# RWKV attention and a maxout layer on one core: the weights' upper halves cast by GpSimd into dense words, the first keys placed by VectorE, the squares of the first chunks taken at the end

## The chip, the cores and the metric

The kernel runs on one core of one Trainium2 chip. The metric is the device time of one execution in microseconds; lower is better.

## The reference

A linear attention with decay (batch 4, 8 heads, 768 tokens, 48 features a head) feeds a feed-forward layer that takes the maximum of three products:

```python
for t in range(S):
    kt, vt, rt = (k[:, :, t], v[:, :, t], r[:, :, t])
    cur = np.einsum('bhd,bhe->bhde', u[None] * kt, vt)
    y[:, :, t] = np.einsum('bhd,bhde->bhe', rt, state + cur)
    state = w[None, :, :, None] * state + np.einsum('bhd,bhe->bhde', kt, vt)
...
x = np.ascontiguousarray(attn_out.transpose(0, 2, 1, 3)).reshape(B * S, H * D)
h = np.maximum(np.maximum(x @ w1, x @ w2), x @ w3)
return (h @ w_out).astype(np.float32)
```

x is 3072 x 384, w1 to w3 are 384 x 768 and w_out is 768 x 384, all four in 64-bit floats; r, k and v are 32-bit.

## The kernel before, in words

**Staging.** The tokens go in 12 chunks of 64 (for all 4 batches, so 256 columns a chunk). A chunk's attention goes in two halves q of 4 heads. For each half SyncE loads `feat` (keys and receptances with the features on partitions) and `tok` (k, r, v with the tokens on partitions). The decay is folded in by scaling `feat`. TensorE makes `scores` (keys by receptances), `values` (the masked scores `am` by v, and the state by r) and `keys` (k by v, added to `state`), in PSUM tiles `psa`. The output of `values` is split into `xh` (rounded, ScalarE, L465) and `xl` (the remainder, VectorE, L470), which are the input of the layer. There each of 6 blocks f has three `psm` groups of 9 matmuls (L487), from `xh` and `xl` and the weights' parts `wh` and `wl`. ScalarE copies the first product to `m`, VectorE takes the maximum with the others (L502), ScalarE rounds it to `hh` and GpSimd, for most blocks of chunk 1 on (VectorE in chunk 0), leaves the remainder `hl` (L511). The `down` product goes from `hh` and `hl` to `io` (ScalarE, L534) and out, by a transfer that ScalarE issues.

**Accuracy.** Attention works in float16 pairs: a high part made by ScalarE (`kd`, `vd`, `ktd`, `sd`, `rh`, `ah`) and a low part by VectorE (the same names, and `rl`, `al`). SyncE then spreads them into block-diagonal tiles (`kb`, `vb`, `ktb`, `sb`) by way of two transfers each. Chunk 0 goes another way: its products are in float32 (`full`, L482), and ScalarE places keys, values and k directly by `apart` (L476, two instructions of 64 partitions).

**Weights.** There are 8 weight blocks n, each in two halves h, 16 loads of 576 KB into four `raw64` buffers. A 64-bit word becomes a 32-bit one in three steps: ScalarE casts its top 16 bits from bfloat16 to float16 into `ztop` (`tops`, L239), VectorE shifts the middle 32 bits and ORs the top in (`convert`, L243), ScalarE rounds to `wh` or `woh` (`round_up`, L246), and VectorE leaves the remainder `wl` (`leave`, L250).

**Checks.** The fast way holds only for inputs of an ordinary size. ScalarE sums the squares of r, k, v and the state of each chunk (`square_sum`, L349, into `stat`), and looks at the weights' words again near the end. `check` makes `good` of it, TensorE counts it (L566), and `flag` decides whether the general way runs behind.

**Order.** Every step is named to a planner, `Plan`, with a due time (counted in chunks), a cost, what it reads and writes and which buffers it takes. The planner lists them for each engine by earliest start and due time; a table `SHIFT` moves the due times of each kind of step, in the opening and later. Each engine then runs its list strictly in order. So does the queue in which SyncE issues loads and spreads.

Of the kernel before, what the change touches and what calls it, by code (L numbers as in the profile page):

```python
# [7 lines left out]
F32 = mybir.dt.float32  # L8
# [10 lines left out]
P = 128  # L19
B, H, S, D = 4, 8, 768, 48  # L20
C = 64
# [16 lines left out]
class Plan:  # L38
# [8 lines left out]
        "act ah": (-5.31, -0.9), "act am": (2.08, 0), "act hh": (1.37, 0.4), "act his": (-0.69, 0), "act io": (-5.36, -2.55),  # L47
        "act kb": (-1.33, 0), "act kdh": (-2.9, 1.2), "act ktb": (1.56, 0), "act ktdh": (2.65, 0.45), "act m": (0.81, -0.9),
        "act odd": (0, 0.6), "act rh": (1.04, -0.85), "act sdh": (-5.26, 2.75), "act sq": (-6.83, 0.2), "act state": (-3.36, 0),
        "act tkt": (-0.31, 0), "act vb": (-2.77, 0), "act vdh": (-3.65, 2.05), "act xh": (1.12, -1.45), "act ztop": (-4.35, 0),  # L50
        "dve a": (4.95, 2.4), "dve al": (5.58, 0.7), "dve am": (-3.84, 0.85), "dve ends": (0, 0.45), "dve flag": (0, -2),
        "dve good": (0, -3), "dve hl": (2.63, -2.25), "dve kT": (6.29, 0), "dve kdec": (8.61, 0), "dve kdl": (-1.52, -0.15),
        "dve ktdl": (-3.55, 1.1), "dve lo": (-4.52, 0), "dve m": (-2.24, 0.3), "dve rT": (9.32, 0), "dve rl": (-2.27, 0.75),
        "dve sdl": (3.31, -0.15), "dve state": (-2.75, 1.5), "dve vdl": (4.98, 0.55), "dve vet": (0, -0.15), "dve word": (-1.81, 0),
# [96 lines left out]
def kernel(ctx, tc, feat, tok, wu, ut, ws, wo, cst, out):  # L151
# [80 lines left out]
    def halves(raw, k):  # L232
        return raw[:, 0:4 * HN].rearrange("p (n four) -> p n four", four=4)[:, :, k]
# [4 lines left out]
    def tops(h, raw):  # L238
        nc.scalar.copy(out=ztop[h].bitcast(F16).rearrange("p (n two) -> p n two", two=2)[:, :, 1], in_=halves(raw[:, 1:], 3).bitcast(BF16))  # L239

    def convert(h, raw):

        nc.vector.scalar_tensor_tensor(out=mids(raw), in0=mids(raw), scalar=13, in1=ztop[h], op0=ALU.logical_shift_right, op1=ALU.bitwise_or)  # L243

    def round_up(n, h, raw):
        nc.scalar.copy(out=part_of(n, h)[0], in_=mids(raw).bitcast(F32))  # L246

    def leave(n, h, raw):
        hi, lo = part_of(n, h)
        nc.vector.tensor_tensor(out=lo, in0=mids(raw).bitcast(F32), in1=hi.bitcast(F32), op=ALU.subtract)  # L250
# [226 lines left out]

    def full(name, q, block, n, w, src):
        t = raws[0, q]
        ps = t[name] = psa.tile([P, U, n], F32, name="psa")  # L480
        for i in range(U):
            nc.tensor.matmul(out=ps[0:w, i, :], lhsT=block.wide[:, i, 0:w], rhs=src[:, i, :], start=True, stop=True)  # L482
# [199 lines left out]
    def act(columns):  # L682
        return 0.11 + 0.83e-3 * columns

    def weight(n, h, due):
        w = ("word", n, h)

        def fetch():
            T[w] = load_weight(n, h, 1)

        dma(due, fetch, 8 * P * HN, takes=[("raw64", w)])
        do(due - 0.05, "act", act(HN), lambda: tops(h, T[w]), reads=[w], writes=[("ztop", h)])
        do(due, "dve", dve(HN), lambda: convert(h, T[w]), reads=[("ztop", h)], writes=[w], near=0.55)
        do(due + 0.05, "act", act(HN), lambda: round_up(n, h, T[w]), reads=[w], writes=[("his", n, h)])
        do(due + 0.1, "dve", dve(HN), lambda: leave(n, h, T[w]), reads=[w, ("his", n, h)], writes=[("lo", n, h)], near=0.6)
# [33 lines left out]
    def before_mask(c, q, due):  # L729
# [6 lines left out]
        squares(c, q, due - 0.15)  # L736
# [234 lines left out]
```

## Time and profile before

| | |
|---|---|
| time, median of 3 runs (lowest to highest) | 416.89 us (416.0 to 417.54) |
| profiled execution: time, span | 418.29 us, 416.4 us |
| TensorE (PE) busy | 392.5 us, 94% |
| VectorE (DVE) busy | 282.5 us, 68% |
| ScalarE (ACT) busy | 256.7 us, 62% |
| GpSimd (POOL) busy | 183.3 us, 44% |
| data moved by DMA | 90.13 MB |

Engines carry short names in the profile: PE for TensorE, PEld its weight load, DVE for VectorE, ACT for ScalarE, POOL for GpSimd, SP for SyncE. L243 is line 243 of the kernel before. A row names line, engine, operation, and then `out<-in` by tiles without their numbers, with partitions x elements. Behind a bar come the busy time and the mean duration of one in ns, and then the time that the engine sat idle right before such an instruction, with what ended it. In a list of waits the three numbers are the time in all in us, how many times, and the longest. In a timeline they are the start and the duration in us; brackets hold the idle time before and its releaser. A stage row gives the stretch, its length, the busy time of PE, PEld, DVE, ACT and POOL with instruction counts, the granted TensorE clock, the share of the DMA engines and GB/s.

### The profile page before, as it was taken

What the parts mean: (1) busy time and instruction counts of PE and PEld (TensorE: products, weight loads), DVE (VectorE), ACT (ScalarE), POOL (GpSimd) and SP (SyncE); (2) the same over time, 40 slices, a digit from 0 to 9 for tenths busy, and PEclk for the clock granted to TensorE, in tenths of its full rate; (3) what the DMA queues carried; (4) which work ended last, traced back from release to release, by engine and by line L of the source; (5) the groups of instructions that cost most, each with busy time, mean ns of one, the idle gap of its engine ahead of it and who ended that gap; (6) DMA issues with size and microseconds to landing.
All of it is one profiled execution on the core that took longest, in us unless ns stands there. A gap on an engine that the chain in (4) does not pass through costs nothing.

```text
span 416.4 us, 11971 instructions
## 1 busy us (share of the span) xinstructions
PE 392.5 (94%) x4758; PEld 387.9 (93%) x4758; DVE 282.5 (68%) x551; ACT 256.7 (62%) x674; POOL 183.3 (44%) x180
## 2 busy tenths in 40 slices
PE   2869899999899999999999999999999999999995
PEld 2759899998799999999999999999999999999995
DVE  6888999987597676666666666566666596353240
ACT  5999987884666566466456456456466477365331
POOL 9000000288469575664664664674654651020120
PEclk9999999999999999999999999999999999999999
DMA  8799998889799897884876885875886996885001
GB/s 287 312 320 210 272 285 279 230 236 251 187 273 262 224 245 175 246 216 131 259 202 145 258 212 149 244 211 150 244 213 148 309 302 146 250 287 216 25 3 44
DMA packets 30959, 90.13 MB, mean 216 GB/s; under 512 B 4784, under 2 KB 9648, under 8 KB 30896
## 3 DMA queue, kind: packets, MB, share of 16 engines
q1 hardware_dynamic: 25568, 84.47, 71.6%
q10 hardware_dynamic: 5328, 4.82, 3.7%
q8 instruction: 39, 0.64, 0.7%
q14 instruction: 24, 0.20, 0.2%
HBM read 45.85 MB, written 4.72 MB: 121 GB/s over the span
## 4 chain that ended last, share of the span: by engine, by line
PE 80%; ACT 9%; DVE 4%; DMA 3%; issue 2%; POOL 1%; ACTq 0%; DVEq 0%; POOLq 0%
PE psm L487 67%; PE psa L409 12%; DMA tok<-in_tok_dram 3%; ACT junk L349 2%; ACT ztop L239 1%; ACT wh L246 1%; ACT kb L476 1%; DVE kd L337 1%; ACT kd L332 0%; ACT ktb L476 0%; DMA wu_sb<-in_wu_dram 0%; ACT xh L465 0%; ACT am L397 0%; DVE al L429 0%; POOL am L385 0%
## 5 line engine op out<-in xcount | busy, mean ns | idle before, releaser
L487 PE MATMUL psm<-xh,wh 128*128 128x256 f32 x648 | 166.3, 286 | 6.2 <-ACT xh L465 2.9
L487 PE MATMUL psm<-xl,wh 128*128 128x256 f32 x648 | 163.4, 282 | 1.1 <-DVE xl L470 1.1
L487 PEld LDWEIGHTS psm<-xh,wh 128*128 128x128 f32 x648 | 123.3, 190 | 6.7 <-ACT xh L465 3.1
L487 PEld LDWEIGHTS psm<-xl,wh 128*128 128x128 f32 x648 | 122.8, 189 | 1.4 <-DVE xl L470 1.4
L487 PE MATMUL psm<-xh,wl 128*128 128x256 f32 x648 | 112.6, 283 | 0.0
L502 DVE TENSOR_TENSOR m<-psm,m 128x256 f32<-128x256 f32 x144 | 60.4, 420 | 64.0 <-PE psm L487 56.8
L487 PEld LDWEIGHTS psm<-xh,wl 128*128 128x128 f32 x648 | 92.7, 190 | 0.0
L366 POOL TENSOR_TENSOR feat<-feat,wrt 128x512 f32<-128x512 f32 x36 | 47.6, 1331 | 74.9 <-PE psm L487 69.0
L511 POOL TENSOR_TENSOR hl<-m,hh 128x256 fp32r<-128x256 f32 x55 | 46.5, 847 | 72.3 <-ACT hh L505 72.1
L505 ACT CAST hh<-m 128x256 fp32r<-128x256 f32 x72 | 28.8, 404 | 56.3 <-DVE m L502 55.8
L487 PE MATMUL psm<-hh,woh 128*128 128x256 f32 x216 | 54.3, 284 | 0.0
L487 PE MATMUL psm<-hh,wl 128*128 128x256 f32 x216 | 53.4, 279 | 0.0
L385 POOL TENSOR_TENSOR am<-tok,u_sb 128x384 f32<-128x384 f32 x18 | 20.9, 1159 | 59.6 <-DVE al L429 59.6
L349 ACT ACTIVATE junk<-tok 128x384 bf16<-128x384 f32 x72 | 37.4, 520 | 11.2 <-DMA tok<-in_tok_dram 9.6
L487 PEld LDWEIGHTS psm<-hh,woh 128*128 128x128 f32 x216 | 40.6, 188 | 0.0
L487 PEld LDWEIGHTS psm<-hh,wl 128*128 128x128 f32 x216 | 40.6, 188 | 0.0
L470 DVE SCALAR_TENSOR_TENSOR xl<-psa,xh 32x256 fp32r<-32x256 f32 (+2 forms) x60 | 28.3, 471 | 13.9 <-ACT xh L465 12.9
L465 ACT ACTIVATE xh<-psa 32x256 fp32r<-32x256 f32 (+2 forms) x60 | 25.0, 417 | 17.0 <-PE psa L409 16.0
L487 PE MATMUL psm<-hl,woh 128*128 128x256 f32 x216 | 35.1, 280 | 0.0
L409 PE MATMUL psa<-ah,vb 128*128 128x64 f16 x352 | 32.9, 194 | 0.0
L409 PE MATMUL psa<-rh,sb 128*128 128x64 f16 x352 | 32.5, 193 | 0.0
L498 ACT COPY m<-psm 128x256 f32<-128x256 f32 x72 | 26.3, 367 | 9.5 <-PE psm L487 8.1
(99 smaller groups left out, 734.7 us busy)
## 6 DMA issues: line engine op xcount, KB each, us to landing
tok<-in_tok_dram SPq DMA_DIRECT2D x24, 576.0 KB, 6.7
raw<-in_ws_dram SPq DMA_DIRECT2D x24, 576.0 KB, 7.3
feat<-in_feat_dram SPq DMA_DIRECT2D x24, 512.0 KB, 5.4
kb<-kd SPq DMA_DIRECT2D x22, 256.0 KB, 5.8
kb<-kd SPq DMA_DIRECT2D x22, 248.0 KB, 6.0
ktb<-ktd SPq DMA_DIRECT2D x20, 256.0 KB, 3.2
ktb<-ktd SPq DMA_DIRECT2D x20, 248.0 KB, 4.3
raw<-in_wo_dram SPq DMA_DIRECT2D x8, 576.0 KB, 5.5
```

Of the source, the lines that this page charges most:

```text
L239: nc.scalar.copy(out=ztop[h].bitcast(F16).rearrange("p (n two) -> p n two", two=2)[:, :, 1], in_=halves(raw[:, 1:], 3).bitcast(BF16))
L349: nc.scalar.activation(out=junk, in_=src, func=AF.Square, scale=scale, accum_out=stat[:, kind, 2 * c + q:2 * c + q + 1])
L366: helper(c).tensor_tensor(out=t[n], in0=t[n], in1=tb, op=ALU.mult)
L385: helper(c).tensor_tensor(out=w.rearrange("p (g b) d -> p g b d", g=2), in0=t["r"], in1=by_token(u_sb, q), op=ALU.mult)
L409: nc.tensor.matmul(out=ps, lhsT=l[i], rhs=rr[j], start=first and n == 0, stop=last and n == 2)
L465: nc.scalar.mul(out=hi, in_=src, mul=SC_X)
L470: nc.vector.scalar_tensor_tensor(out=lo, in0=src, scalar=SC_X, in1=hi.bitcast(F32), op0=ALU.mult, op1=ALU.subtract)
L487: nc.tensor.matmul(out=ps, lhsT=a, rhs=b, start=first and n == 0, stop=last and n == len(prods) - 1)
L498: nc.scalar.copy(out=m, in_=ps)
L502: nc.vector.tensor_tensor(out=to, in0=ps, in1=m, op=ALU.max)
L505: nc.scalar.copy(out=h[0][:, f, :], in_=m)
L511: lows_by(c, f).tensor_tensor(out=h[1][:, f, :], in0=m, in1=h[0][:, f, :].bitcast(F32), op=ALU.subtract)
```

## The change

There are four edits and a new `SHIFT` table.

- `tops` goes from ScalarE to GpSimd: 16 casts of 128x576.
- `convert` writes to one of two new dense tiles `word` instead of back into `raw64`, where the words stood 8 bytes apart; `round_up` and `leave` read the dense word. A `raw64` buffer is free after `convert`, no longer only after `leave`.
- In chunk 0 the scaled keys are written straight into their places in `kb` by VectorE (`scale_apart`, two products of 64x8x64 for each half), instead of scaled by VectorE (128x512) and placed by ScalarE.
- The 12 square sums of r, k and v in chunks 0 and 1 leave the start. `squares_again` loads the four `tok` tiles a second time (576 KB each, not before chunk 10's layer has begun) and takes the sums then.

```diff
-        "act ah": (-5.31, -0.9), "act am": (2.08, 0), "act hh": (1.37, 0.4), "act his": (-0.69, 0), "act io": (-5.36, -2.55),
+        "act ah": (-7.54, -0.9), "act am": (7.01, 0), "act hh": (1.5, 0.4), "act his": (-2.1, 0), "act io": (1.62, -2.55),
...
     def tops(h, raw):
-        nc.scalar.copy(out=ztop[h].bitcast(F16).rearrange("p (n two) -> p n two", two=2)[:, :, 1], in_=halves(raw[:, 1:], 3).bitcast(BF16))
+        nc.gpsimd.tensor_copy(out=ztop[h].bitcast(F16).rearrange("p (n two) -> p n two", two=2)[:, :, 1], in_=halves(raw[:, 1:], 3).bitcast(BF16))
+
+    word = [const.tile([P, HN], I32, name=f"word{h}") for h in range(2)]

     def convert(h, raw):
-        nc.vector.scalar_tensor_tensor(out=mids(raw), in0=mids(raw), scalar=13, in1=ztop[h], op0=ALU.logical_shift_right, op1=ALU.bitwise_or)
-    def round_up(n, h, raw):
-        nc.scalar.copy(out=part_of(n, h)[0], in_=mids(raw).bitcast(F32))
+        nc.vector.scalar_tensor_tensor(out=word[h], in0=mids(raw), scalar=13, in1=ztop[h], op0=ALU.logical_shift_right, op1=ALU.bitwise_or)
+    def round_up(n, h):
+        nc.scalar.copy(out=part_of(n, h)[0], in_=word[h].bitcast(F32))
...
-        nc.vector.tensor_tensor(out=lo, in0=mids(raw).bitcast(F32), in1=hi.bitcast(F32), op=ALU.subtract)
+        nc.vector.tensor_tensor(out=lo, in0=word[h].bitcast(F32), in1=hi.bitcast(F32), op=ALU.subtract)
...
+    def scale_apart(q):
+        for hh in range(2):
+            to = kb.wide[HS[hh], :, hh * C:(hh + 1) * C].rearrange("p (g b) n -> p g b n", g=2)
+            nc.vector.tensor_tensor(out=to, in0=raws[0, q]["kT"][HS[hh]], in1=wkt[HS[hh], 2 * q:2 * q + 2].unsqueeze(2).broadcast_to([C, 2, B, C]), op=ALU.mult)
...
-        do(due - 0.05, "act", act(HN), lambda: tops(h, T[w]), reads=[w], writes=[("ztop", h)])
-        do(due, "dve", dve(HN), lambda: convert(h, T[w]), reads=[("ztop", h)], writes=[w], near=0.55)
+        do(due - 0.05, "pool", 0.9, lambda: tops(h, T[w]), reads=[w], writes=[("ztop", h)])
+        do(due, "dve", 0.72, lambda: convert(h, T[w]), reads=[w, ("ztop", h)], writes=[("word", h)], near=0.55)
...
+    def squares_again(c, q, due):
+        w = ("again", c, q)
+        def fetch():
+            T[w] = raw.tile([P, 3, 2, B, D], F32, name="tok")
+            nc.sync.dma_start(out=T[w], in_=tok[c, q])
+        dma(due, fetch, 589824, reads=[("begun", NCH - 2)], takes=[("tok", w)])
+        for kind, i in enumerate((1, 0, 2)):
+            do(due + 0.3, "act", act(U * D) + 0.1, lambda kind=kind, i=i: square_sum(units(T[w][:, i]), kind, c, q), reads=[w], writes=[("sq", c, q, kind)])
...
-        squares(c, q, due - 0.15)
+        if c > 1:
+            squares(c, q, due - 0.15)
...
-        do(due - 0.30, "dve", dve(U * C), lambda: scale(c, q, "kT"), reads=[f], writes=[("kT", c, q)], near=0.55)
-        do(due - 0.29, "act", 1.25, lambda: apart(kb, units(raws[c, q]["kT"]), C), reads=[("kT", c, q)], writes=["kb"])
+        do(due - 0.30, "dve", 2 * dve(U * C), lambda: scale_apart(q), reads=[f], writes=["kb"], near=0.55)
...
+    for k in range(4):
+        squares_again(k // 2, k % 2, NCH - 1.2 + 0.15 * k)
```

How the order moves is shown at three places. A row is the line (of the kernel that it belongs to; behind the new lines they stand up to 20 further down), the operation, `out<-in` and the shape. The first place is the opening on ScalarE. Before, behind the turned copies `tkt`:

```order
L301 ACTIVATE tkt<-psa 64x192 x2
L476 ACTIVATE kb<-feat 64x8x64 x2
L349 ACTIVATE junk,stat<-tok 128x384 x2
L476 ACTIVATE vb_137<-tok 64x8x48 x2
L349 ACTIVATE junk,stat<-tok 128x384 x3
L476 ACTIVATE vb_139<-tok 64x8x48 x2
L349 ACTIVATE junk,stat<-tok 128x384
L239 CAST ztop_109<-raw_177 128x576
L476 ACTIVATE kb<-feat 64x8x64 x2
L239 CAST ztop_110<-raw_179 128x576
```

After, from the same instruction:

```order
L302 ACTIVATE tkt<-psa 64x192 x2
L477 ACTIVATE vb_139<-tok 64x8x48 x2
L477 ACTIVATE vb_141<-tok 64x8x48 x2
L477 ACTIVATE ktb<-tok 64x8x48 x2
L247 CAST wh<-word_113 128x576
L444 ACTIVATE state<-psa 112x192 x2
L477 ACTIVATE ktb<-tok 64x8x48 x2
L333 ACTIVATE sd<-state 128x8x48
L350 ACTIVATE junk,stat<-state 128x384
L247 CAST wh<-word_114 128x576
```

The placements of `kb`, the square sums and the casts `ztop` are gone from ScalarE, and the placements of v and k and the roundings `wh` have moved up.

The second place is VectorE's list at the end of chunk 1's attention, up to the last `xl` of that chunk. Before:

```order
L250 TENSOR_TENSOR wl_106<-raw_503,wh 128x576
L511 TENSOR_TENSOR hl<-m,hh 128x256
L337 TENSOR_TENSOR ktd<-tok,ktd 128x8x48
L445 SCALAR_TENSOR_TENSOR state<-state,wc,psa 128x192 x2
L470 SCALAR_TENSOR_TENSOR xl<-psa,xh 96x256
L470 SCALAR_TENSOR_TENSOR xl<-psa,xh 32x256 x3
L243 SCALAR_TENSOR_TENSOR raw_643<-raw_643,ztop_109 128x576
```

After:

```order
L446 SCALAR_TENSOR_TENSOR state<-state,wc,psa 128x192 x2
L338 TENSOR_TENSOR ktd<-tok,ktd 128x8x48
L508 TENSOR_TENSOR m<-psm,m 128x256
L340 SCALAR_TENSOR_TENSOR sd<-state,sd 128x8x48
L244 SCALAR_TENSOR_TENSOR word_113<-raw_567,ztop_109 128x576
L508 TENSOR_TENSOR m<-psm,m 128x256
L471 SCALAR_TENSOR_TENSOR xl<-psa,xh 96x256
L471 SCALAR_TENSOR_TENSOR xl<-psa,xh 32x256 x3
L251 TENSOR_TENSOR wl_107<-word_113,woh 128x576
```

In the new order one more `sd`, one more weight word and an `m` stand ahead of the `xl`, and they are of those that stood behind it.

The third place is SyncE's list around the loads of chunk 3's second half, with the spreads of chunk 2. Before:

```order
L319 DMA vb_139<-vd_147 64x1536
L320 DMA vb_139<-vd_147 64x1488
L319 DMA kb<-kd 64x2048
L320 DMA kb<-kd 64x1984
L319 DMA ktb<-ktd 64x2048
L320 DMA ktb<-ktd 64x1984
L174 DMA feat<-in_feat_dram 128x1024
L179 DMA tok<-in_tok_dram 128x1152
L174 DMA feat<-in_feat_dram 128x1024
L319 DMA kb<-kd 64x2048
L320 DMA kb<-kd 64x1984
L179 DMA tok<-in_tok_dram 128x1152
```

After, from the load of chunk 3's first half on:

```order
L174 DMA feat<-in_feat_dram 128x1024
L179 DMA tok<-in_tok_dram 128x1152
L174 DMA feat<-in_feat_dram 128x1024
L320 DMA kb<-kd 64x2048
L321 DMA kb<-kd 64x1984
L320 DMA vb_141<-vd_149 64x1536
L321 DMA vb_141<-vd_149 64x1488
L320 DMA sb_155<-sd 64x1536
L321 DMA sb_155<-sd 64x1488
L320 DMA ktb<-ktd 64x2048
L321 DMA ktb<-ktd 64x1984
L179 DMA tok<-in_tok_dram 128x1152
```

Before, the first `feat` and `tok` are of chunk 3's second half, the second `feat` and the last `tok` of chunk 4's first. After, the second `feat` and the last `tok` are of chunk 3's second half. In the new order the `feat` of chunk 3's second half is issued together with the first half's loads, ahead of the eight spreads, and its `tok` stays right behind the spread of `ktb`.

On GpSimd the 16 casts stand behind the clears of the start and ahead of the first `hl`; the library load, an instruction without operands, stood between the clears and the first scaling, and now stands between the last cast and that `hl`.

More of the change, by code (lines that the diff above doesn't have):

```diff
@@ L51 @@
[L51 to L54, printed above, removed]
[5 rows of a table removed]
+        "act ah": (-7.54, -0.9), "act am": (7.01, 0), "act hh": (1.5, 0.4), "act his": (-2.1, 0), "act io": (1.62, -2.55),
@@ new lines @@
+        "act kb": (-1.33, 0), "act kdh": (-8.51, 1.2), "act ktb": (-4.5, 0), "act ktdh": (4.46, 0.45), "act m": (-2.86, -0.9),
+        "act odd": (0, 0.6), "act rh": (0.2, -0.85), "act sdh": (-4.6, 2.75), "act sq": (-3.89, 0.2), "act state": (-7.43, 0),
+        "act tkt": (3.33, 0), "act vb": (-5.29, 0), "act vdh": (-3.58, 2.05), "act xh": (-1.59, -1.45), "act ztop": (-4.35, 0),
+        "dve a": (1.88, 2.4), "dve al": (5.06, 0.7), "dve am": (-11.06, 0.85), "dve ends": (0, 0.45), "dve flag": (0, -2),
@@ new lines @@
+        "dve good": (0, -3), "dve hl": (3.66, -2.25), "dve kT": (6.71, 0), "dve kb": (-0.7, 0), "dve kdec": (6.89, 0),
+        "dve kdl": (-8.79, -0.15), "dve ktdl": (-9.44, 1.1), "dve lo": (-1.24, 0), "dve m": (3.3, 0.3), "dve rT": (7, 0),
+        "dve rl": (-0.7, 0.75), "dve sdl": (4.81, -0.15), "dve state": (-10.3, 1.5), "dve vdl": (2.04, 0.55), "dve vet": (0, -0.15),
+        "dve word": (0.2, 0), "dve xl": (-7.56, 0.55), "pe count": (0, -1.9), "pe dn": (-10.07, 0.1), "pe ke": (-0.59, 0.1),
@@ L60 @@
+        "pe sc": (-5.03, -0.3), "pe turned": (-2.07, 0), "pe up": (-1.28, 0), "pe va": (-2.16, -0.15), "pool am": (0, -0.75),
+        "pool hl": (-1.67, -1.2), "pool kT": (0, -0.6), "pool kdec": (0, 0.35), "pool rT": (0, -0.9), "pool ztop": (-0.78, 0),
+        "sp feat": (-7.21, 0.15), "sp kb": (6.19, 1.7), "sp ktb": (-1.09, -0.9), "sp sb": (-3.8, -0.85), "sp tok": (-3.9, -0.55),
+        "sp vb": (-3.12, 1.4), "sp vet": (0, 0.45), "sp word": (2.19, 0),
     }
@@ L691, in weight @@
         dma(due, fetch, 8 * P * HN, takes=[("raw64", w)])
[L692 to L695 removed]
+        do(due - 0.05, "pool", 0.9, lambda: tops(h, T[w]), reads=[w], writes=[("ztop", h)])
+        do(due, "dve", 0.72, lambda: convert(h, T[w]), reads=[w, ("ztop", h)], writes=[("word", h)], near=0.55)
+        do(due + 0.05, "act", act(HN), lambda: round_up(n, h), reads=[("word", h)], writes=[("his", n, h)])
+        do(due + 0.1, "dve", dve(HN), lambda: leave(n, h), reads=[("word", h), ("his", n, h)], writes=[("lo", n, h)], near=0.6)
     def again(n, h, due):
```

5 lines of the change are left out of this document (1 added, 4 removed), and 5 rows, old and new, of the table SHIFT.

## The prediction

> **What bounds the kernel now.** I read three views in this order: the stages of the span (busy time of each engine between two times), TensorE's list of waits, and the groups by line. The stages first. The columns are the stretch, its length, and for each engine the busy time and the count of instructions; TensorE's weight load (PEld) can be passed over.
>
> ```profile
> 5.40:29.20 23.80, 17.02 (x85) 15.96 (x85) 20.73 (x35) 21.34 (x50) 5.58 (x8) 1.00 0.89 336
> 29.20:42.70 13.50, 11.10 (x76) 10.45 (x76) 11.66 (x21) 13.33 (x35) 0.00 (x0) 1.00 0.93 226
> 42.70:62.20 19.50, 19.48 (x271) 19.35 (x272) 18.65 (x40) 17.17 (x41) 0.00 (x0) 1.00 0.97 286
> 62.20:80.70 18.50, 18.50 (x195) 18.41 (x194) 17.77 (x37) 14.33 (x37) 0.71 (x1) 1.00 0.82 243
> 80.70:119.10 38.40, 33.96 (x496) 33.13 (x496) 29.18 (x47) 26.66 (x77) 27.95 (x25) 1.00 0.89 234
> 119.10:411.70 292.60, 292.43 (x3641) 290.59 (x3641) 181.72 (x363) 161.89 (x436) 144.24 (x136) 1.00 0.72 201
> 345.00:380.00 35.00, 35.00 (x460) 34.82 (x459) 17.80 (x40) 20.07 (x50) 4.42 (x6) 1.00 0.76 236
> ```
>
> From 119.10 to 411.70 TensorE (PE) works without a gap, and the change takes no matmul away. So only what happens before 119.10 can move the end: there TensorE lacks 6.78 us up to 29.20, 2.40 up to 42.70 and 4.44 between 80.70 and 119.10. In the two stretches from 42.70 to 80.70 it is full, but VectorE (DVE) is busy 36.42 of 38.00 us beside it. I take VectorE as the tighter of the two there: its list of work decides when chunk 1's input is ready. ScalarE (ACT) is busy 21.34 of 23.80 and 13.33 of 13.50 us in the opening. GpSimd (POOL) does nothing from 29.20 to 62.20. What TensorE waited for:
>
> ```profile
> PE psa L295 <- DVE stat L345: 5.4, 1, 5.4
> PE psm L487 <- ACT xh L465: 2.9, 1, 2.9
> PE psa L482 <- ACT kb L476: 2.3, 2, 2.1
> PE psm L487 <- ACT io L534: 2.0, 1, 2.0
> ...
> PE psa L409 <- DMA kb<-kd: 0.9, 1, 0.9
> PE psa L409 <- DVE al L429: 0.8, 1, 0.8
> PE psa L409 <- DVE rl L376: 0.8, 1, 0.8
> ```
>
> The first 5.4 us are the start, which the change leaves alone. The waits for kb and xh are the opening; io, kb<-kd, al and rl are the four gaps between 80.70 and 119.10.
>
> **The change part by part.** The costs, from the groups by line (busy time, then mean ns of one):
>
> ```profile
> L243 DVE SCALAR_TENSOR_TENSOR raw<-raw,ztop 128x576 int32<-128x576 int32 x16 | 12.1, 755 | 2.1 <-issue 1.3 <-ACT ztop L239 0.5
> L366 DVE TENSOR_TENSOR feat<-feat,wrt 128x512 f32<-128x512 f32 x12 | 8.0, 683 | 0.5 <-DMA feat<-in_feat_dram 0.5
> L239 ACT CAST ztop<-raw 128x576 f16<-128x576 bf16 x16 | 13.6, 848 | 0.1
> L476 ACT ACTIVATE kb<-feat 64x512 f32<-64x512 f32 x4 | 2.5, 626 | 0.0
> L349 ACT ACTIVATE junk<-tok 128x384 bf16<-128x384 f32 x72 | 37.4, 520 | 11.2 <-DMA tok<-in_tok_dram 9.6 <-ACT io L534 0.9
> L349 ACT ACTIVATION_READ_ACCUMULATOR junk<-tok 128x1 f32 x72 | 13.5, 188 | 0.0
> ```
>
> ScalarE loses 16 casts (13.6 us), 4 placements of keys (2.5 us) and, in the start, 12 square sums with their read-outs (12 x 0.708, 8.5 us by these means). That is 24.6 us off an engine that was full, so it stops being a limit before 80.70, and the keys, `xh` and the first `psm` group wait for it no longer. TensorE's 2.3 and 2.9 us go. What is late next there is VectorE, and the gain is what VectorE lets through.
>
> VectorE's list is therefore the first term. I count its instructions in both orders from the first scaling to the `xl` of chunk 1's second half, which ends the list for chunk 1. The new list has 4 placements of keys (64x8x64) in place of 2 scalings of 128x512, and through reordering one `sd`, two `m` and one weight word more ahead of that `xl`. These rows end the list now, and give the durations and the two waits that I expect to stay:
>
> ```profile
> 60.00 1.75 DVE L470 SCALAR_TENSOR_TENSOR xl<-psa,xh 96x256 fp32r<-96x256 f32 x4 [0.26 <-ACT xh L465]
> 57.00 0.42 DVE L502 TENSOR_TENSOR m<-psm,m 128x256 f32<-128x256 f32 x1 [0.15 <-PE psm L487]
> 27.48 0.56 DVE L339 SCALAR_TENSOR_TENSOR sd<-state,sd 128x384 f16<-128x384 f32 x1
> 5.86 1.29 DVE L366 TENSOR_TENSOR feat<-feat,wrt 128x512 f32<-128x512 f32 x2 [0.47 <-DMA feat<-in_feat_dram]
> 12.30 0.72 DVE L419 COPY_PREDICATED am<-cs,psa 128x512 f32<-128x512 int32 x1 [0.45 <-PE psa L482]
> ```
>
> Two scalings in a row took 1.29, so one fills about 0.60 of the queue when the next follows (1.29 less the mean 0.683). In the same way I take 0.47 for `sd`, 0.33 for `m` and 0.67 for a word, each some 0.09 under its duration. A placement has 8x64 elements on half the partitions; no row shows that form, and I take 0.60, the scaling of the same length (bounds 0.3, half, since half the data, to 0.68). Added: 4 x 0.60 - 2 x 0.60 + 0.47 + 2 x 0.33 + 0.67 = 3.0 us. VectorE was busy 51.04 of the 56.80 us from 5.40 to 62.20, 0.45 of which lies behind the `xl` that ends at 61.75. So the new list is 50.59 + 3.0 = 53.6 us long. Its waits now come to 5.76. With ScalarE free I let only the two above stay, 0.9 us (bounds 0.5 and 3). It then ends at 5.40 + 53.6 + 0.9 = 59.9 instead of 61.75: **1.9 us gained**, between 2.3 and a loss of 0.2.
>
> The second term is what the casts on GpSimd cost VectorE. No row has a cast on GpSimd, but GpSimd works beside VectorE twice in the trace, and the two differ:
>
> ```profile
> 7.25 0.56 DVE L385 TENSOR_TENSOR am<-tok,u_sb 128x384 f32<-128x384 f32 x1
> 7.29 0.75 POOL L312 MEMSET sd<- 128x784 f32 x1
> ...
> 94.26 3.06 POOL L366 TENSOR_TENSOR feat<-feat,wrt 128x512 f32<-128x512 f32 x2 [1.01 <-DVE ktd L337]
> 94.67 1.51 DVE L511 TENSOR_TENSOR hl<-m,hh 128x256 fp32r<-128x256 f32 x1
> ...
> 58.00 0.42 DVE L511 TENSOR_TENSOR hl<-m,hh 128x256 fp32r<-128x256 f32 x1
> L376 DVE TENSOR_TENSOR rl<-feat,rh 128x512 f16<-128x512 f32 x22 | 23.3, 1061 | 0.1
> L337 DVE TENSOR_TENSOR ktd<-tok,ktd 128x384 f16<-128x384 f32 x20 | 13.1, 656 | 2.9 <-ACT ktd L332 2.9
> L230 POOL MEMSET ztop<- 128x576 f32 x2 | 1.1, 577 | 0.3 <-POOLq L958 0.3
> ```
>
> Beside a memset, which reads nothing, VectorE's product takes its usual 0.56. Beside GpSimd's scaling, which reads two operands, a difference that takes 0.42 alone took 1.51: 1.09 lost in 1.51 of overlap, the worst case. Two groups give the average: the 22 `rl` lie beside GpSimd's arithmetic for 14.0 us in all and take 1.061, though the shortest takes 0.68, so 0.60 lost per us; the 20 `ktd`, 10.2 us beside it and 0.656 against 0.54, lose 0.23. I take 0.47 per us for arithmetic with two operands. A cast reads one operand, so I take the middle, 0.24. Its own length lies between the memset of as many elements, 0.577, and the scaling's 1.53 (3.06 for two); I take 0.9, near ScalarE's 0.848. About two thirds of VectorE's time goes to instructions with two operands. A cast then costs 0.9 x 0.67 x 0.24 = 0.14, and the 13 ahead of that `xl` cost **1.8 us** (bounds 0 and, at 0.47, 3.7; at the worst pair's 0.72, 5.6; a full exclusion, 13 x 0.6, gives 7.8).
>
> The Trainium skill, "GPSIMD Engine Reference", section 1 (Specifications), says that GpSimd shares its SBUF interfaces with VectorE, and that VectorE's instructions with two SBUF inputs suffer from it; the words, the remainders and the new placements are all of that kind, so the rule speaks against this change. The trace agrees on the pair at 94.67 and not on the one at 7.25. By its section 3.1, a tight loop of about 1.8 cycles per element, a cast of 576 elements would take an estimated 0.86 us, and the sum would then be 0.1 us better.
>
> The third term is the four gaps between 80.70 and 119.10. These rows show two of them from the other side:
>
> ```profile
> 81.31 1.64 DVE L339 SCALAR_TENSOR_TENSOR vd<-tok,vd 128x384 f16<-128x384 f32 x1
> 83.47 1.21 DVE L429 TENSOR_TENSOR al<-am,ah 128x512 f16<-128x512 f32 x1
> 94.31 11.67 DMA tok<-in_tok_dram
> 103.26 0.37 ACT L534 COPY io<-psm 128x256 f32<-128x256 f32 x1 [2.82 <-DMA kb<-kd]
> 106.44 0.52 ACT L349 ACTIVATE junk<-tok 128x384 bf16<-128x384 f32 x1 [2.81 <-DMA tok<-in_tok_dram]
> tok<-in_tok_dram SPq DMA_DIRECT2D x24, 576.0 KB, 6.7
> ```
>
> `al` was late because GpSimd's first scaling stretched `vd` and `al`. In the new order that scaling stands behind two `hl`, and VectorE has 1.7 us less to do between the `xl` above and that `al`, since the rows counted above were pulled ahead. So that gap of 0.8 goes. TensorE's 2.0 come from ScalarE, which stood twice for 2.8 us between two `io`, where it issues the output's transfers: first until a kb<-kd had landed, then until chunk 4's first `tok`, issued at 94.31, landed at 106, 11.7 us instead of the usual 6.7. These two stand in SyncE's (SP's) list as before, and the output still comes behind them. But the `feat` of chunk 3's second half is issued ahead of eight spreads instead of right before them: 524 KB fewer in the crowd, 2.2 us at that stretch's 234 GB/s. I let the 2.0 go by it, leave kb<-kd and rl, and charge 0.6 for new trouble: 0.8 + 2.0 - 0.6 = **2.2 us gained** (bounds 0 and 3.6, the gaps of 0.8, 2.0 and 0.8 all shut).
>
> The rest at nothing. The buffers of a weight load come free after the word and not after the remainder, which lets later loads start earlier; VectorE decides, not they. The dense word has the same 576 elements: 0 (bounds -0.08 x 28, the stride's possible price, and 0). GpSimd's library load moves from behind the memsets to behind the last cast; it has until the first `hl` of chunk 1. Its cover gone, it delays one `hl`. The 4 reloads of `tok` and 12 squares come near the end:
>
> ```profile
> L570 DVE TENSOR_SCALAR flag<-psa x1: 136/136/136, 401.2 to 401.2; 1x1 int32<-1x1 f32 x1
> ```
>
> Between 345 and 380 ScalarE is busy 20.07 of 35, and 8.5 more fit; 2.36 MB at that stretch's 236 GB/s are 10 us of a load that was 0.76, so the queues come near to full. The squares feed `good`, for which TensorE's count waits in order, 90 matmuls before the last, and the flag stands at 401.2, 10.5 before the last matmul. Behind a square that waits for its reload, ScalarE holds `m`, `hh` and `io`. I take 0; bounds 0 and 1.5.
>
> **The sum.** 1.9 - 1.8 + 2.2 = 2.3 us. The profiled execution took 418.29 us, 1.40 over the median of 416.89; so 416.0 of its kind, and **414.6** against the median. Half a per cent, what can be told from no change, is 2.1 us: 414.8 to 419.0.
>
> **The rivals.** B, the casts cost VectorE nothing, as the memset's row says: 1.8 us back, 412.8; with no wait left in the opening and all four gaps shut, 410.7. Against it: a memset reads nothing.
>
> C, the other side: each cast shuts VectorE's two-operand instructions out for its whole length. 13 x 0.6 = 7.8 instead of 1.8, so 6.0 us later: 420.6. It decides from 0.32 us a cast, where the two gains of 4.1 are used up, and the kernel is measurably slower from 0.48. For it speaks the pair at 94.67, 0.72 lost per us; against it, `ktd` with 0.23.
>
> D, the gaps in chunks 2 and 3 come again, in other places: VectorE is as full as before, the transfers are at a share of 0.89, and one late `tok` still holds `io`. The third term is 0: 416.8.
>
> E, the late squares hold ScalarE's queue or the count: TensorE waits for a reload of 6.7 us with perhaps half of it uncovered, 3.3 us: 417.9.
>
> **How the numbers follow.** The forecast 0.44, B 0.20, C 0.12, D 0.20, E 0.04. The forecast's own range is 412.8 to 416.4 (each term 0.6 us off, all one way). Above 0.5% faster are nearly all of B and 0.28 of the forecast: 0.47. Within it, 0.16 of the forecast, 0.18 of D, 0.02 of E, 0.02 of C: 0.38. Slower, the rest: 0.15. The range of 8 in 10 leaves out most of C, E and B's tip: 410.8 to 418.8.
>
> **What would show it.** Right: the wait for kb under 0.5 us; TensorE's first `psm` group at 28 to 29 us instead of 29.19, followed by the others without a break; chunk 1's last `xl` ended at about 61.7; VectorE's words and remainders at 0.8 to 1.0 beside casts of about 0.9; no 2.0 wait for `io`. Casts without effect on the words point to B, words of 1.2 and more to C. The prediction is wrong if VectorE is not what decides from 30 to 62 us: if the words wait for weight loads, or the remainders for ScalarE, then the first term is not 1.9; and if a wait stands in the tail behind 345 us, the fourth is not nothing.

## The result, and the profile after

The changed kernel took 423.94 us (median of 4 runs, 423.41 to 425.53) against 417.22 us for the kernel before: 1.6% slower, ratio 1.0164 with a 95% interval of 1.0134 to 1.0195. The forecast was 414.6 us, and the range ended at 418.8. The profiled execution took 425.53 us. A ratio takes of each kernel only the runs within 1.5% of its fastest (the longer ones count as a slower state), while medians are over all runs, so the two can differ. Line numbers below are the changed kernel's. First its stages, in the same columns and stretches as before:

```profile
5.40:29.20 23.80, 20.09 (x101) 19.08 (x101) 23.19 (x34) 12.25 (x27) 12.14 (x14) 1.00 0.96 361
29.20:42.70 13.50, 11.84 (x99) 11.79 (x100) 13.33 (x25) 9.35 (x29) 3.92 (x4) 1.00 1.00 278
42.70:62.20 19.50, 15.96 (x212) 15.01 (x212) 18.88 (x35) 9.51 (x21) 4.24 (x4) 0.91 0.66 206
62.20:80.70 18.50, 17.22 (x159) 16.67 (x156) 17.94 (x34) 12.94 (x37) 2.15 (x2) 1.00 0.80 219
80.70:119.10 38.40, 35.78 (x500) 35.16 (x497) 32.12 (x52) 27.12 (x80) 29.74 (x26) 0.96 0.89 249
119.10:411.70 292.60, 289.94 (x3645) 288.20 (x3644) 184.05 (x363) 168.00 (x458) 143.21 (x136) 0.99 0.74 209
```

ScalarE's load did fall, from 51.84 to 31.11 us between 5.40 and 62.20. But VectorE is now busy 55.40 of these 56.80 us, and TensorE, full between 42.70 and 62.20 before, lacks 3.54 us there. Behind 119.10, where it had no gap before, it lacks 2.66 us. The granted clock, 1.00 before in all these stretches, is 0.91, 0.96 and 0.99 in three of them. TensorE's list of waits:

```profile
PE psa L296 <- DVE hl L288: 5.4, 1, 5.4
PE psa L410 <- DMA ktb<-ktd: 4.6, 2, 2.7
PE psa L410 <- DVE al L430: 3.2, 3, 2.2
PE psm L493 <- DVE xl L471: 3.2, 2, 1.9
PE psa L488 <- issue: 1.9, 2, 1.5
PE psa L488 <- DVE am L420: 1.5, 1, 1.5
PE psm L493 <- DVE wl L251: 0.8, 1, 0.8
PE psm L493 <- DVE m L508: 0.2, 1, 0.2
```

The waits for ScalarE's kb, xh and io are gone. VectorE (al, xl, am, wl: 8.7 us; 3.6 before for xl, am, al and rl) stands in their place, and a transfer, ktb<-ktd, that TensorE had not waited for before. The group of the casts, from the groups by line (count, then busy time and mean ns of one):

```profile
L239 POOL CAST ztop<-raw 128x576 f16<-128x576 bf16 x16 | 16.9, 1065 | 41.1 <-DVE word L244 31.8
```

Some of them in the timeline (start, duration), with VectorE's instructions beside them and the last `xl` of chunk 1:

```profile
19.20 2.36 POOL L239 CAST ztop<-raw 128x576 f16<-128x576 bf16 x2 [2.36 <-DVE word L244]
19.73 1.14 DVE L340 SCALAR_TENSOR_TENSOR sd<-state,sd 128x384 f16<-128x384 f32 x1
20.79 1.33 DVE L251 TENSOR_TENSOR wl<-word,wh 128x576 fp32r<-128x576 f32 x1
...
29.96 1.75 DVE L471 SCALAR_TENSOR_TENSOR xl<-psa,xh 96x256 fp32r<-96x256 f32 x4
30.10 0.84 POOL L239 CAST ztop<-raw 128x576 f16<-128x576 bf16 x1 [4.75 <-DVE word L244]
...
36.65 1.22 POOL L239 CAST ztop<-raw 128x576 f16<-128x576 bf16 x1 [2.10 <-DMA raw<-in_ws_dram]
37.07 1.15 DVE L386 TENSOR_TENSOR am<-tok,u_sb 128x384 f32<-128x384 f32 x1
...
64.32 1.75 DVE L471 SCALAR_TENSOR_TENSOR xl<-psa,xh 96x256 fp32r<-96x256 f32 x4
```

`sd` takes 1.14 beside a cast and 0.55 alone, the remainder `wl` 1.33 instead of 0.75, `am` 1.15 instead of 0.56. The `xl`, with one operand in PSUM, takes its 1.75 beside a cast as well as alone. Summed over all of VectorE's instructions beside the casts ahead of chunk 1's last `xl`, the time over their lone durations is 6.2 us. That `xl` ends at 66.07 instead of 61.75. TensorE's longest wait for VectorE behind the opening, and its two waits for ktb, in the timeline:

```profile
51.61 0.19 PE L410 MATMUL psa<-al,vb 128*128 128x64 f16 x1 [2.20 <-DVE al L430]
...
109.40 0.38 PE L410 MATMUL psa<-vd,ktb 128*128 128x48 f16 x9 [1.97 <-DMA ktb<-ktd]
...
136.51 0.25 PE L410 MATMUL psa<-vd,ktb 128*128 128x48 f16 x3 [2.65 <-DMA ktb<-ktd]
```

And the stretches of 5 us behind the two waits for ktb, where the last three columns are the granted clock, the share of the DMA engines and GB/s:

```profile
110.00:115.00 5.00, 5.00 (x41) 4.96 (x37) 3.69 (x9) 4.87 (x16) 2.83 (x3) 0.66 0.57 175
135.00:140.00 5.00, 3.49 (x41) 3.49 (x42) 3.38 (x9) 4.88 (x15) 0.00 (x0) 0.80 0.53 137
140.00:145.00 5.00, 5.00 (x39) 5.00 (x39) 4.73 (x6) 2.21 (x8) 2.49 (x2) 0.86 0.57 131
```

Behind each of these two gaps the clock stood at half for 3.4 us. That is 5.00 x 0.34 = 1.7 us lost after the first and 5.00 x (0.20 + 0.14) = 1.7 after the second. TensorE is then without a gap of its own to the end, as before.

### The profile page after: what moved, and what is told of

The parts are those of the page before. It is cut to its first block, busy times and chain, and to the rows that moved or that the text cites. A ratio compares the mean times of both kernels' runs of the same rounds, so it can differ in the third digit from the quotient of the medians.

```text
span 423.8 us, 11990 instructions
## 1 busy us (share of the span) xinstructions
PE 397.9 (94%) x4758; PEld 392.8 (93%) x4758; DVE 293.2 (69%) x553; ACT 242.3 (57%) x654; POOL 200.3 (47%) x196
## 4 chain that ended last, share of the span: by engine, by line
PE 73%; DMA 5%; DVE 4%; issue 0%; SPq 0%; ACT 0%; DVEq 0%
PE psm L493 61%; PE psa L410 12%; DMA ktb<-ktd 5%; DVE feat L367 1%; DVE m L508 0%; DVE al L430 0%; DVE wl L251 0%; DVE kd L338 0%; DVE rl L377 0%; DVE vd L340 0%; DVE am L387 0%; DVE tok L406 0%; DVE am L386 0%; SPq L320 0%; DVE a L391 0%
## 5 line engine op out<-in xcount | busy, mean ns | idle before, releaser
L493 PE MATMUL psm<-xl,wh 128*128 128x256 f32 x648 | 165.3, 284 | 3.2 <-DVE xl L471 3.2
L493 PE MATMUL psm<-xh,wh 128*128 128x256 f32 x648 | 168.0, 288 | 0.2 <-DVE m L508 0.2
L493 PEld LDWEIGHTS psm<-xl,wh 128*128 128x128 f32 x648 | 124.2, 192 | 4.0 <-DVE xl L471 4.0
L493 PEld LDWEIGHTS psm<-xh,wh 128*128 128x128 f32 x648 | 124.8, 193 | 0.4 <-ACT wh L247 0.4
L493 PE MATMUL psm<-xh,wl 128*128 128x256 f32 x648 | 114.1, 285 | 0.8 <-DVE wl L251 0.8
L493 PEld LDWEIGHTS psm<-xh,wl 128*128 128x128 f32 x648 | 93.8, 192 | 1.2 <-DVE wl L251 1.1
L517 POOL TENSOR_TENSOR hl<-m,hh 128x256 fp32r<-128x256 f32 x55 | 44.7, 814 | 84.9 <-ACT hh L511 71.6
L367 POOL TENSOR_TENSOR feat<-feat,wrt 128x512 f32<-128x512 f32 x36 | 48.8, 1365 | 8.5 <-DMA feat<-in_feat_dram 8.3
L338 DVE TENSOR_TENSOR kd<-feat,kd 128x512 f16<-128x512 f32 x22 | 21.0, 956 | 22.2 <-ACT kd L333 22.2
L239 POOL CAST ztop<-raw 128x576 f16<-128x576 bf16 x16 | 16.9, 1065 | 41.1 <-DVE word L244 31.8
L504 ACT COPY m<-psm 128x256 f32<-128x256 f32 x72 | 26.4, 366 | 17.1 <-PE psm L493 14.9
```

The costliest lines, as they stand in the source:

```text
L338: nc.vector.tensor_tensor(out=dense.dense[:, 1, :, 0:w], in0=src, in1=dense.dense[:, 0, :, 0:w], op=ALU.subtract)
L367: helper(c).tensor_tensor(out=t[n], in0=t[n], in1=tb, op=ALU.mult)
L493: nc.tensor.matmul(out=ps, lhsT=a, rhs=b, start=first and n == 0, stop=last and n == len(prods) - 1)
L504: nc.scalar.copy(out=m, in_=ps)
L517: lows_by(c, f).tensor_tensor(out=h[1][:, f, :], in0=m, in1=h[0][:, f, :].bitcast(F32), op=ALU.subtract)
```

## The experiments

Theory P: GpSimd's casts hold up VectorE. Theory O: the new order is slower by itself. All ratios are to the kernel before on the same chip.

**e1: the casts back on ScalarE, every other list unchanged.**

```diff
-        nc.gpsimd.tensor_copy(out=ztop[h]..., in_=...)
+        nc.scalar.copy(out=ztop[h]..., in_=...)
```

> The changed kernel with its 16 casts back on ScalarE, every engine's list otherwise as it stands. Theory P (each cast on GpSimd holds up VectorE's instructions with two operands in SBUF, about 0.47 us a cast): VectorE's remainders and products beside a cast fall back to their lone durations, chunk 1's last xl ends at 60 to 61 us instead of 66.07, and the time is 417 to 419.5. Rival O (the new order itself is slower, whoever casts): xl ends at 64 us or later and the time stays at 421.5 to 424.5.

Measured: 421.95 us (417.41 to 424.91, 10 runs), ratio 1.0107 (1.0072 to 1.0142). Between the two theories: VectorE's instructions ahead of chunk 1's `xl` take their lone times again, 6.0 us less in sum than in the changed kernel, but the `xl` moved forward by only 2.85 us, since VectorE now waits for ScalarE's list, in which the casts stand: 1.69 us for a cast at 39.95 and 0.67 for `xh`. The waits for ktb stayed (2.31 and 2.04 us). So the casts on GpSimd are part of the loss and not all of it. The `xl` in e1's timeline:

```profile
61.47 1.76 DVE L471 SCALAR_TENSOR_TENSOR xl<-psa,xh 96x256 fp32r<-96x256 f32 x4 [0.67 <-ACT xh L466]
```

**e2: the kernel before, its lists unchanged, with the casts on GpSimd** (e1's edit, the other way).

> The kernel before with nothing changed but the 16 casts on GpSimd, ScalarE's and VectorE's lists as before. P: VectorE's instructions beside a cast stretch by some 0.5 us, less the waits that they fill; chunk 1's last xl ends 2 to 5 us later than 61.75, time 418.5 to 422. O: ScalarE, full in the opening, loses 13.6 us of work, so the time is 414 to 417.5.

Measured: 416.35 us (413.98 to 417.39, 10 runs), ratio 0.9987 (0.9968 to 1.0005). P's number missed, O's came. Chunk 1's `xl` ends at 59.87 in the profiled execution, which is the fastest of the ten, so earlier than before the edit. In this order VectorE's busy time from 5.40 to 62.20 rose from 51.04 to 54.32, and it had waited 5.76 us there, so most of the 3.3 went into its waits. TensorE's wait for xh fell from 2.9 to 2.3. What the casts took from VectorE, ScalarE's relief gave back. The three stages of the opening:

```profile
5.40:29.20 23.80, 17.24 (x86) 16.23 (x86) 22.61 (x38) 19.91 (x49) 13.63 (x15) 1.00 0.93 349
29.20:42.70 13.50, 13.50 (x98) 13.46 (x99) 12.70 (x22) 11.39 (x34) 1.79 (x2) 1.00 0.91 237
42.70:62.20 19.50, 18.84 (x268) 18.61 (x266) 19.01 (x39) 12.88 (x34) 6.25 (x6) 1.00 0.99 276
```

**e3: e1, with GpSimd clearing the tile ahead of each cast of ScalarE.**

```diff
+        nc.gpsimd.memset(ztop[h].bitcast(F32), 0.0)
         nc.scalar.copy(out=ztop[h]..., in_=...)
```

> e1, with GpSimd clearing the same tile (128x576, writes only) ahead of each of ScalarE's casts, so that GpSimd works at the same places of the order as in the changed kernel but reads nothing, and the chain to the word is longer than there. P (what costs is GpSimd's reading beside VectorE's): as e1 to within 1.5 us. Rival L (the price is the longer way to the word, or any work of GpSimd): 421 to 425, like the changed kernel.

Measured: 422.35 us (419.71 to 424.11, 5 runs), ratio 1.0108 (1.0072 to 1.0144), practically e1's. The number alone lies in L's range too, as e1's does; the traces decide. The memsets take 0.58 us each, and VectorE's instructions ahead of chunk 1's last `xl` take the same time as in e1, to 0.02 us in sum. GpSimd at work without reading costs nothing that shows, nor does the longer way to the word.

**e4: e1, with GpSimd casting 448 of each 576 into a tile that nobody reads.**

```diff
         nc.scalar.copy(out=ztop[h]..., in_=...)
+        nc.gpsimd.tensor_copy(out=spare, in_=halves(raw[:, 1:], 3).bitcast(BF16)[:, 0:448])
```

> e1, with GpSimd casting 448 of each 576 upper halves a second time into a tile that nothing reads. The chain to the word is e1's; only GpSimd's reading is back. P: VectorE's instructions beside these casts stretch by 0.35 to 0.5 us each, time 3 to 6 us over e1, 420.5 to 424. L: as e1 to within 1 us, since nothing waits for the spare casts.

Measured: 425.94 us (425.18 to 426.46, 4 runs), ratio 1.0214 (1.0182 to 1.0247), 4.0 us over e1. That is P's difference to e1, though over its range of times. Chunk 1's `xl` starts 3.2 us later than in e1: VectorE's instructions ahead of it take 2.3 us longer in sum, up to 0.40 each, and the rest is mostly waits. Nothing waits for these casts' result, so it is the casting beside VectorE that costs. L falls. How much of the 4.0 us comes by way of the clock isn't separated: up to the last matmul it stood at half for 10.2 us in e4's trace and for 3.4 in e1's.

**e5: the changed kernel with no casts at all.** The weights' top 16 bits are left out.

```diff
-        nc.gpsimd.tensor_copy(out=ztop[h]..., in_=...)
+        pass
```

> The changed kernel without the 16 casts at all (the top 16 bits of the weights are left out, so the layer computes with other weights); nothing stands in for them on ScalarE. P (the casts hold up VectorE, by 6.2 us of stretched instructions ahead of chunk 1's last xl): that xl ends at 59.5 to 61 us instead of 66.07, and the time is 4 to 6 us under the changed kernel's, 418 to 420; what is left over the kernel before, 1 to 3 us, is the order's. Rival O alone (the casts cost nothing to speak of): 422 to 424.5.

Measured: 419.79 us (414.15 to 423.64, 10 runs), 4.15 under the changed kernel. Five runs lie up to 418.26 and five from 421.32 on; the ratio, 0.9994 (0.9961 to 1.0028), is that of the lower five. The profiled execution is the fastest one; its `xl` in the timeline:

```profile
57.64 1.76 DVE L471 SCALAR_TENSOR_TENSOR xl<-psa,xh 96x256 fp32r<-96x256 f32 x4
```

It ends at 59.40, 6.67 us before the changed kernel's. VectorE's list is the same there, instruction by instruction, and in the changed kernel none of it waits for a cast; its durations are 6.1 us shorter in sum here, its waits 0.4. So P holds for VectorE's list in place and size. Of TensorE's waits for ktb one of 1.8 us is left.

**e6: all the edits in the old order.** The functions of the kernel before are exchanged and its lists kept; the early squares are left out and their sums set. With only two `word` tiles, some words are overwritten in this order before their remainder is taken, so some weights are wrong.

```diff
-        ... lambda: scale(c, q, "kT") ...
-        ... lambda: apart(kb, units(raws[c, q]["kT"]), C) ...
+        ... lambda: scale_apart(q) ...
+        ... lambda: None ...
```

> The kernel before with its own due times and its lists as they stand, but with the edits put into their places: casts on GpSimd, dense words, chunk 0's keys placed by VectorE, and the squares of chunks 0 and 1 left out (their sums are set to an allowed value; the late ones are left out too). Theory O (the new due times bring the two waits for ktb at 109 and 136 us and the halved clock behind them, 4 to 8 us): without them the edits are worth something, 411 to 415.5, and no wait for ktb over 0.5 us stands in the trace. Rival (the edits themselves cost, whatever the order): 418.5 to 423.

Measured: 421.38 us (418.9 to 422.07, 8 runs), ratio 1.0095 (1.0067 to 1.0123). The number is the rival's, but it doesn't tell the theories apart, by a fault of the experiment: the second half's keys now go straight into the one tile `kb`, and in the old order they stand ahead of the work on the first half's scores. VectorE waits there for TensorE (its timeline), and TensorE then waits 5.3 us for `am`:

```profile
12.13 1.64 DVE L484 TENSOR_TENSOR kb<-feat,wrt 64x512 f32<-64x512 f32 x2 [2.14 <-PE psa L490]
```

**e7: the changed kernel without the late squares** (the four calls of `squares_again` left out, the sums set to an allowed value).

> The changed kernel with the four late loads of tok and their 12 squares left out (the sums are set to an allowed value). All theories held so far: TensorE has no wait behind 140 us, so the time stays within 1.5 us of the changed kernel's, 422 to 425. Rival E (they hold ScalarE or the transfers at the end): 419 to 421.5.

Measured: 424.08 us (419.45 to 424.71, 4 runs), ratio 1.0122 (1.0056 to 1.0189). No gain over the changed kernel is seen, though the interval is wide; and the changed kernel's trace has no wait of TensorE behind 140 us. Rival E falls.

**e8: ktb ahead of tok at two places of SyncE's list.**

```diff
+    for c in (4, 5):
+        p = <the load of tok, chunk c, first half>; behind = <SyncE's next step, the spread of ktb>
+        order.remove(p)
+        order.insert(order.index(behind) + 1, p)
```

> The changed kernel with one exchange at two places of SyncE's list: the spread of ktb goes ahead of the tok load that stood right before it (chunk 4's and chunk 5's first tok, issued at 99.24 and 123.28). O by way of the transfers: ktb lands 2 to 4 us earlier, the waits of 1.97 and 2.65 us go or fall under 1 us, the halved clock behind them (3.4 us at half, 1.7 us each) goes too, and the time falls by 3 to 7 us, to 417 to 421. Rival (the crowd of transfers only shifts: tok comes later instead and holds ScalarE): 422 to 425.

Measured: 422.29 us (420.54 to 425.75, 4 runs), ratio 1.0118 (1.0049 to 1.0188). Both waits went (0.3 us of ktb is left) and the clock stayed up behind 100 us. The last `xl` of chunk 5 came 1.65 us earlier than in the changed kernel; but in between there is a new gap, so the gain is unclear, and the time is the rival's. TensorE's timeline:

```profile
158.78 0.38 PE L493 MATMUL psm<-xh,wh 128*128 128x256 f32 x1 [2.47 <-DVE m L508]
```

**e9: spare matmuls in the two gaps of the changed kernel.**

```diff
+        for _ in range({(2, 1): 12, (3, 1): 18}.get((c, q), 0)):
+            nc.tensor.matmul(out=<the keys' tile>, lhsT=wup[:, 0, 0, 0, :], rhs=<256 columns of wup>, start=True, stop=True)
```

> The changed kernel with spare matmuls ahead of the keys of chunk 2's and chunk 3's second halves, which waited 1.97 and 2.65 us for ktb: 12 and 18 of 128x256 (0.117 us each, 1.4 and 2.1 us), into the tile that the keys then overwrite. Theory H (after a gap of about 2 us TensorE's granted clock stands at half for some 3.4 us, which costs 1.7 us each time): the two waits shrink to about 0.6 us, no slice from 105 to 145 us has a granted clock under 0.95, and the time falls by 2 to 4 us, to 420 to 422. Rival (the clock falls whatever TensorE does, or the fall is hidden): 423 to 425.

Measured: three runs of 420.75 to 424.34 and one of 768.47 that I can't explain; median of the four 423.26, ratio 1.0112 (1.0068 to 1.0155). The clock is as H has it, in the same stretches as above:

```profile
110.00:115.00 5.00, 5.00 (x69) 4.91 (x67) 3.26 (x8) 4.46 (x13) 2.46 (x3) 1.00 0.65 161
135.00:140.00 5.00, 4.45 (x57) 4.25 (x55) 3.52 (x9) 4.88 (x15) 0.00 (x0) 1.00 0.79 187
140.00:145.00 5.00, 5.00 (x45) 5.00 (x44) 5.00 (x7) 2.96 (x9) 3.78 (x3) 1.00 0.61 161
```

This execution began 2.5 us late (TensorE's first wait 7.9 instead of 5.4). Its last `io` starts at 417.34, 1.4 us before the changed kernel's 418.78 in spite of that. From the start of chunk 1's last `xl` (65.86) to there it took 351.48 us, 3.0 less than the changed kernel. The clock's part is shown; that the runs are faster by 2 to 4 us is not.

**e11: e5 with the same spare matmuls.**

> e5 (the changed kernel without its casts, whose runs lay between 414 and 424) with the same spare matmuls. H (the spread is the halved clock behind those waits, which some runs meet and others do not): the upper runs go, 414 to 419, median 415.5 to 418. Rival (the spread has another cause): median 419 to 421.5 and runs over 421 as in e5.

Measured: 418.45 us (415.19 to 421.57, 10 runs) against e5's 419.79, ratio 1.0022 (0.9986 to 1.0057) against e5's 0.9994 (0.9961 to 1.0028). The uppermost runs are gone, but the two can't be told apart, and neither theory's median came. In this execution chunk 1's `xl` starts at 61.47 instead of e5's 57.64, behind waits of TensorE for `hh` (1.5 us) and ktb (1.3) near 54 us and a half clock from 54.81 on, long before the spare matmuls. So the spread has a share before 60 us as well.

**e10: the kernel before in its own order, with casts on GpSimd and late squares.**

> The kernel before with its own due times and lists, with two of the edits: casts on GpSimd and the squares of chunks 0 and 1 late; the words stay strided and ScalarE still places the keys. It asks whether these two edits are worth anything where the new order is not taken. Theory P and O: e2 with a further 7.7 us off ScalarE in the opening, so the waits for xh and kb shrink by 1 to 2 us; 414 to 416.5, 0 to 2.5 us under the kernel before. Rival (VectorE, held up by the casts, gives nothing back): 416.5 to 419.

Measured: 417.26 us (415.62 to 418.59, 12 runs), ratio 1.0008 (0.9987 to 1.0029). No difference: the rival's number. No version here beats the kernel before.

**e12: the changed code with the old due times, listed anew.**

> The changed kernel's code with the due times of the kernel before (the two new kinds of step take the times of those that they replace), listed anew by the planner. It splits the loss between the edits and the new table. If the new table carries it (theory O alone): 414 to 417. If the casts on GpSimd carry it (P): VectorE's instructions beside the casts stretch here too, by 5 to 7 us in sum ahead of chunk 1's last xl, which ends after 63 us, and the time is 419 to 425. A wait for ktb over 1.5 us behind 100 us would say that these waits come with VectorE's lateness and not with the table; none would say that the table brings them.

Measured: 428.53 us (427.21 to 430.7, 4 runs), ratio 1.026 (1.0207 to 1.0314). The `xl` ends at 70.37. Both ranges were missed. There is no wait for ktb behind 100 us. TensorE has other long ones instead, the first two in the opening, the last at 98.87:

```profile
PE psa L488 <- ACT ktb L477: 6.0, 1, 6.0
PE psa L488 <- DVE am L420: 4.5, 1, 4.5
PE psm L493 <- DVE xl L471: 2.7, 1, 2.7
PE psa L410 <- DMA kb<-kd: 2.5, 1, 2.5
```

The new due times are worth 4 to 4.6 us to these edits (by the ratios and by the medians). By what was said ahead of the run, they bring the long waits for ktb; short ones stand in the old lists with casts on GpSimd too (1.0 us in e10, 0.7 in e6). Without the new due times the edits are worse still. O, as a theory that the table carries the loss, falls.

## Why the prediction was wrong, step by step

**What bounds.** Right in part. VectorE's list decides from 30 to 62 us: the first `psm` matmul came at 28.38, as forecast, but the next waited 1.92 us for an `xl`. It was wrong that only what happens before 119.10 can move the end: of the two waits for ktb the longer, 2.65 us at 136.51 with 1.7 us of half clock behind it, lies after that. Nothing behind 145 us adds to the loss.

**First term, VectorE's list.** Right in e5. I had its end at 59.9 without any price for the casts; e5, which has none, ends it at 59.40. That is the fastest of its runs, so in part luck: in e11, with the same code up to there, the list ends at 63.22, since VectorE waits there for TensorE, which waits for `hh` and ktb. The keys' placements took 1.39 for two, against the 1.29 of two scalings.

**Second term, the casts.** This is the step that failed first. I priced a cast at 0.14 us, 1.8 for 13; the changed kernel shows 6.2, and e5 gives 6.67 for the end of the list. 59.9 and 6.2 make 66.1, where the trace has 66.07. Done over again from the changed kernel's trace, the product is this: ahead of that `xl` stand 14 casts of 14.9 us in all, where 13 of 0.9 make 11.7; 11.6 us of it, 0.78 and not two thirds, lie beside instructions with two operands in SBUF, words aside; and 6.2 us lost in 11.6 are 0.53 per us where I had 0.24. The halving is the largest of these errors. One operand read instead of two was no reason for it: a `wl` and an `sd` beside a pair of casts lost 0.58 and 0.59, and with 0.47 unhalved my own product gave 3.7. (The 0.47 isn't the mean of its two groups either: weighted by their overlap they give 0.44, which moves the term by 0.1.) Spread over the 13 casts that I counted, 6.2 us are 0.48 each. This is rival C at the very price from which I had it measurably slower, with a chance of 0.12. The row of the memset, which spoke for no price, doesn't carry over, as e3 and e4 show together: clearing costs nothing, casting into a tile that nobody reads costs 4.0 us.

The Trainium skill's sentence in "GPSIMD Engine Reference", section 1, on two SBUF inputs of VectorE is borne out by these rows but for some words, and it makes no difference there between one operand and two on GpSimd's side; I made that difference without a row for it. Its section 3.1 gave an estimated 0.86 us for a cast; the trace has 0.84 where VectorE was on an `xl`, and 1.07 on the average.

**Third term, the gaps in chunks 2 and 3.** Failed, and with the wrong sign. The gaps for io, kb<-kd and rl did close and al's shrank to 0.65. But the keys of the second halves now reach TensorE before their ktb has landed: 1.97 and 2.65 us. Each gap was followed by a half clock, 1.7 us each, which e9's spare matmuls kept away. From the start of chunk 1's last `xl` to the start of the last `io` the kernel before took 411.70 - 60.00 = 351.70 us and the changed one 418.78 - 64.32 = 354.46: 2.8 lost where I had 2.2 gained. Without the half clock (e9, one trace) the same stretch took 351.48, 0.2 gained. So about 3 of the 5.0 us are the clock's, for which the prediction had no term; the rest goes by the waits for ktb, which took back what the closed gaps gave. I had followed the one transfer that was late before, and not the ones that the new order makes urgent; e8, where ktb is issued ahead of a `tok`, has 0.3 us of these waits left. This is rival D's mechanism, at more than D's price, and it came together with C, while I had priced each rival alone.

**Fourth, the rest at nothing.** Not contradicted: TensorE has no wait behind 140 us in the changed kernel, and a word takes its 0.75 us as before.

**The sum.** The two failed terms account for the miss: 4.4 us in the second (6.2 for 1.8) and 5.0 in the third make 9.4; 423.94 less 414.6 is 9.3. That it closes is no proof of the third term, which was measured as all that is left behind the `xl`. How far it depends on the casts is open in part: the two traces without them took 349.94 us (e5, 407.58 - 57.64) and 350.08 (e11, with the spare matmuls, 411.55 - 61.47), which is 1.8 and 1.6 gained, near the 2.2 forecast. But e5's runs lie between 414 and 424, and with the casts on ScalarE (e1) it was 352.90, 1.2 lost.

## What to carry to other kernels

Work taken off a full engine is worth only what the engine beside it can use: look at how busy that one is, and whether the move itself takes time from it. Price a move to GpSimd beside VectorE from the rows where the two stand side by side, and by what will stand next to it in the new order, without a discount that no row shows. And ask of each gap of some 2 us on TensorE whether the clock will fall behind it: here that made it cost nearly 4.

## What the runs showed of the hardware

- A GpSimd cast of 128x576 from bfloat16 to float16 takes 0.84 us beside an `xl` and up to 1.33 (the second of the pair at 46.84) beside VectorE's two-operand instructions, which themselves mostly lose 0.47 to 0.60 each. VectorE's instructions with an operand in PSUM lose nothing, nor does a reduction (0.54 at 15.86), nor a word with a cast beside it for 0.6 us (at 19.06).
- TensorE's granted clock fell to half for 3.41 us after gaps of 1.97, 2.20 and 2.65 us in the changed kernel, beginning 1.1 to 1.5 us after it had gone on; matmuls of 128x256 then started every 0.213 us instead of 0.117. After the gap of 2.01 us that ended at 108.01 in the kernel before it stayed at 1.00, so the length alone doesn't decide. What does can be read from the places of the falls, 52.70, 110.72 and 138.03: they lie 17 and 8 times 3.413 us apart, and wherever another trace has more than one fall, they too lie whole multiples of it apart. Cut the span into slices of 3.41 us by that step (columns as in the stages):

```profile
107.31:110.72 3.41, 1.44 (x31) 1.35 (x31) 0.42 (x2) 2.38 (x8) 0.99 (x1) 1.00 0.89 237
110.72:114.13 3.41, 3.41 (x18) 3.41 (x18) 3.21 (x8) 3.28 (x11) 1.96 (x2) 0.50 0.53 174
```

TensorE lacks 1.97 of 3.41 us in the first slice, and the second is at half. In the kernel before the step, set by a fall at 414.38 behind its last matmul, cuts the gap of 2.01 in two:

```profile
103.76:107.18 3.42, 2.25 (x20) 2.04 (x18) 0.74 (x1) 0.71 (x3) 0.41 (x2) 1.00 1.01 263
107.18:110.59 3.41, 2.58 (x39) 2.53 (x40) 1.23 (x3) 2.94 (x9) 0.94 (x1) 1.00 0.38 128
```

It lacks 1.17 and 0.83, and the clock stays. In all 14 traces, from 40 to 400 us, every slice at full clock in which TensorE lacked 1.66 us or more was followed by one at half, and none in which it lacked 1.56 or less. The same cut spares the gap of 2.31 us in e1 and that of 2.47 in e8. The step lies elsewhere in each execution, so whether a gap of 2 us costs another 1.7 is chance from run to run. In the opening it doesn't hold: gaps up to 5.4 us bring no fall on record there, while the matmuls start every 0.213 us (31.24 to 35.56 in the changed kernel) at a granted clock of 1.00.
- The Trainium skill, "TensorE: Matmul & The Clock Gate", Part 1, has the half rate come back after an idle window of about 3.4 us; here gaps well under that did it, and the half rate then lasted about as long as such a window.
